# First-layer weights of two experts loaded as column halves over two depth blocks, the rest asked for behind two gathers

## The chip, the cores and the metric

The kernel runs on one core of one Trainium2 chip. The metric is the device time of one execution in microseconds, given as the median of several runs. Engines are PE (TensorE, matrix products), DVE (VectorE), ACT (ScalarE), POOL (GpSimd) and SP (SyncE, which only issues transfers here); transfers go through DMA queues.

## The reference

The kernel computes block-causal attention and feeds its result to a mixture of experts with fixed capacity:

```python
# attention: 8 batches, 8 heads, 576 positions of 64, blocks of 64
scores = scale * np.matmul(q, k.transpose(0, 1, 3, 2))
scores = np.where(block_i >= block_j, scores, -1000000000.0)
attn = softmax(scores)                      # exp(s - max) / (sum + 1e-9)
x = np.matmul(attn, v)                      # as x: 4608 tokens x 512
# mixture of experts: N=4608 tokens, D=512, E=8 experts, F=1024, cap=576
logits = x @ w_gate
for idx in np.argsort(-logits.flatten()):   # best (token, expert) pairs first
    tok, e = idx // E, idx % E
    if assigned[tok] < 0 and counts[e] < cap:
        assigned[tok] = e; counts[e] += 1
for e in range(E):
    h = np.maximum(x[assigned == e] @ w1[e], 0.0)
    out[assigned == e] = h @ w2[e]
```

`w1` is 8 x 512 x 1024 and `w2` 8 x 1024 x 512, in float32.

## The kernel before

The first 340 us are attention; its end writes x to DRAM as pairs of float16 values (a high and a low part), 1024 values a token, and leaves the gate's logits in SBUF. The rest is the mixture of experts, taken expert by expert (`k` = 0 to 7, in an order found while it runs).

For each expert but the last, `route` (L710) finds the logit that the 576th token has, by a search of 14 steps. A step is a loop over three engines: DVE makes three candidates (`cd`, L769) and counts with two of them (`jk`, L777), ACT counts with the third (`ja`, L750), a small matmul adds the counts over the partitions (`tot`, L791), and DVE turns them into the next step (`sg`, L794). Before the search PE transposes the logits (`rt`, L741) and ACT copies them to `m_PB` (L745). After it, `po` and `pe` (L852 and L908) and the DVE work between them (L870, L897, L899, L900) turn the chosen tokens into a list of indices `ix`, and a new expert's route may begin.

`gather` (L972) has POOL fetch the 576 rows of x in five indirect transfers `xg` (L980). For experts 0 and 1 `flip` has PE transpose each of them (`xt`, L990), and ACT and DVE copy the result to `X` (L994, L995); later experts use transposing transfers of SP (L1005).

`weights` (L927) fetches an expert's weights on SP's queue as eight pieces `raw` of 128 x 1024 float32, 512 KB each (L966), into six buffers. A piece of w1 (n = 0 to 3) is one block of 128 depths by all 1024 columns; a piece of w2 (n = 4 to 7) two blocks by 512 columns. `conv` splits each into two float16 parts, high and low. For w1 of experts 0 and 1 the high part is one instruction of ACT (L938) and the low part one of DVE (L940); for everything else ACT scales and rounds (L945, L949) and POOL subtracts (L951).

`ffn` (L1008) multiplies. For each group f of 128 columns of w1 and each of four depth blocks d it runs three matmuls `h` (L1030: high by high, high by low, low by high), for expert 0 first for 128 tokens, then for 448, for the others for 256 and 320. ACT takes the result out as `HH` (L1016) and DVE its low part as `HL` (L1018). Then `y` (L1055, L1059) multiplies with w2 for five groups of tokens; `yo` is scaled out and scattered to the output by POOL (L1046). Eight matmuls `warm` (L924) fill the wait for the first gather.

All engines' orders are fixed when the program is built. Each helper is a generator that yields the engine, a cost in ns and the events it needs; a list scheduler `Sched` picks the next by these, and the instructions are written out in that order. So an engine runs its list in sequence and waits in place. `sc.set` and `sc.soft` give the time of an event as the scheduler believes it; `hold` (L886) keeps `po` and `pe` of the last expert back by a fixed time in that schedule. The two lines that say what a set of h matmuls of expert 0 waits for, and what the first piece of w2 of expert 0 does, are

```python
yield T,3*(w/2.4+3),...,('wc',k,d) if k==0 else None      # L1026: depth block d converted
yield G,60,('gi',0); ... nc.gpsimd.memset(raw[:,0:1],0.0)  # L960-962
```

The memset of one column makes that piece's transfer wait for POOL, which runs it behind the fifth gather; SP's queue is in order, so the pieces after it wait too.

## Time and profile before

| | us |
|---|---|
| median of 3 runs | 804.21 |
| the runs | 802.95, 804.21, 807.38 |
| profiled execution, its own time | 801.86 |
| span of the profiled execution | 800.1 |
| PE busy | 717.8 (90%) |
| DVE busy | 585.0 (73%) |
| ACT busy | 545.1 (68%) |
| POOL busy | 467.0 (58%) |

Busy time of an engine is the sum over its instructions; what an engine lacks to the span is idle time, in front of some instruction, and the profile names what released it. The granted clock of PE is given in parts of its full 2.4 GHz. A transfer's time runs from its issue on a queue to its landing. Times below are from the start of the span.

### The profile page before, as it was taken

To read this page: it belongs to the slowest core of one execution; us is meant where nothing else is said; L and a number is where in the kernel's file an instruction comes from. 1 tells how busy PE (TensorE), PEld (TensorE's weight loads), DVE (VectorE), ACT (ScalarE), POOL (GpSimd) and SP (SyncE) were. 2 spreads that over 40 slices of the span, in tenths; PEclk is the share of its full clock that TensorE was granted. 3 is DMA by queue.
4 is the path that set the end of the run, shared out by engine and by line. 5 is a ranking of instruction groups with operands and counts; after the bars stand their busy time and mean duration, and the time that the engine had idled before them with its cause. 6 is when DMAs were issued, how large, how long until landed. Compare 5 with 4: busy or idle time off the path is not lost.

```text
span 800.1 us, 19136 instructions
## 1 busy us (share of the span) xinstructions
PE 717.8 (90%) x6539; PEld 479.6 (60%) x6539; DVE 585.0 (73%) x2395; ACT 545.1 (68%) x1476; POOL 467.0 (58%) x509
## 2 busy tenths in 40 slices
PE   5889998899999999913898999999999999999995
PEld 3666676677767767601644755747557475574752
DVE  6899798988889799488787977969777683730210
ACT  5789888888988888533745859496775947392210
POOL 5788888897889876212324337475471926873001
PEclk9899999999999999955899999999999999999998
DMA  9879999999999991324408049291845819861001
GB/s 203 157 145 179 213 203 209 164 176 204 230 164 222 188 198 35 99 80 133 138 14 294 25 139 231 74 295 42 254 129 184 179 49 273 270 162 40 20 15 45
DMA packets 244305, 121.51 MB, mean 152 GB/s; under 512 B 200816, under 2 KB 227312, under 8 KB 244208
## 3 DMA queue, kind: packets, MB, share of 16 engines
q1 hardware_dynamic: 238320, 101.42, 56.1%
q0 software_dynamic: 5888, 18.88, 7.4%
q8 instruction: 51, 0.84, 0.4%
q14 instruction: 46, 0.38, 0.2%
HBM read 71.32 MB, written 18.87 MB: 113 GB/s over the span
## 4 chain that ended last, share of the span: by engine, by line
PE 58%; DVE 19%; DMA 8%; ACT 8%; issue 3%; POOL 3%; SPq 1%; POOLq 0%; DVEq 0%; ACTq 0%
PE h L1030 23%; PE y L1055 16%; PE psb L463 5%; DVE m L405 5%; PE psb L380 4%; DMA kT<-k 4%; PE psb L498 4%; ACT P L416 4%; DVE kS L350 2%; POOL P L438 2%; PE y L1059 2%; DMA xg<-x,ix 2%; ACT PT L444 2%; DVE jk L776 1%; DMA raw<-in_moe_w_dram 1%
## 5 line engine op out<-in xcount | busy, mean ns | idle before, releaser
L438 POOL TENSOR_TENSOR P<-P,m 128x320 f32<-128x320 f32 (+8 forms) x285 | 209.3, 769 | 48.2 <-DVE m L430 28.4
L1030 PE MATMUL h<-X,W 128*128 128x320 f16 (+3 forms) x1536 | 195.1, 287 | 0.0
L1030 PEld LDWEIGHTS <-W 128*128 128x128 f16 x1536 | 142.2, 98 | 42.7 <-issue 3.1
L416 ACT ACTIVATE P<-psb,m 128x576 f32<-128x576 f32 (+8 forms) x288 | 149.2, 542 | 25.8 <-DVE m L409 19.7
L1055 PE MATMUL y<-W,HH 128*128 128x512 f16 x512 | 152.2, 379 | 0.0
L951 POOL TENSOR_TENSOR W<-raw,W 128x1024 f16<-128x1024 f32 x56 | 118.4, 2136 | 40.6 <-ACT W L949 38.3
L405 DVE TENSOR_REDUCE m<-psb 128x1 f32<-128x576 f32 (+8 forms) x288 | 125.0, 481 | 12.4 <-PE psb L380 11.9
L463 PE MATMUL psb<-mident,P 128*128 128x128 f32 x800 | 106.0, 281 | 10.9 <-POOL P L438 3.6
L1046 POOL DMA_INDIRECT out_dram<-yo,ix x40 | 39.4, 986 | 113.1 <-ACT yo L1038 79.2
L380 PEld LDWEIGHTS <-qT 128*64 128x64 f16 x1408 | 78.1, 112 | 42.8 <-issue 27.8
L380 PE MATMUL psb<-kT,qT 128*64 128x288 f16 (+8 forms) x704 | 91.7, 286 | 10.2 <-ACT P L416 9.7
L463 PEld LDWEIGHTS psb<-mident,P 128*128 128x128 f32 x800 | 87.3, 142 | 22.5 <-POOL P L438 6.4
L498 PE MATMUL psb<-PT,V 128*64 128x448 f32 (+5 forms) x776 | 97.2, 388 | 2.4 <-DVE PT L446 1.9
L980 POOL DMA_INDIRECT xg<-x,ix x40 | 41.6, 1040 | 95.8 <-DVE ix L918 37.7
L1055 PE MATMUL y<-W,HL 128*128 128x512 f16 x256 | 97.0, 379 | 0.0
L1016 ACT ACTIVATE HH<-h 128x320 f16<-128x320 f32 (+3 forms) x128 | 52.1, 410 | 63.9 <-PE h L1030 59.5
L444 ACT ACTIVATE PT<-psb 128x512 f32<-128x512 f32 (+1 forms) x165 | 82.4, 592 | 5.8 <-PE psb L463 5.6
L380 PE MATMUL psb<-kS,qT 128*64 128x288 f16 (+8 forms) x704 | 84.4, 284 | 1.6 <-DVE kS L350 1.5
L1018 DVE SCALAR_TENSOR_TENSOR HL<-h,HH 128x320 f16<-128x320 f32 (+3 forms) x128 | 56.9, 452 | 38.5 <-ACT HH L1016 38.2
L1055 PEld LDWEIGHTS <-HH 128*128 128x128 f16 x512 | 46.9, 98 | 52.6 <-issue 2.0
L945 ACT ACTIVATE raw<-raw 128x512 f32<-128x512 f32 x112 | 67.4, 626 | 6.6 <-DMA raw<-in_moe_w_dram 6.5
L498 PEld LDWEIGHTS psb<-PT,V 128*64 128x64 f32 x776 | 49.5, 137 | 33.5 <-issue 24.3
(204 smaller groups left out, 1074.9 us busy)
## 6 DMA issues: line engine op xcount, KB each, us to landing
raw<-in_moe_w_dram SPq DMA_DIRECT2D x64, 512.0 KB, 5.5
x<-XR SPq DMA_DIRECT2D x8, 1152.0 KB, 5.7
kn<-in_k_dram SPq DMA_DIRECT2D x15, 576.0 KB, 5.1
qn<-in_q_dram SPq DMA_DIRECT2D x15, 576.0 KB, 7.1
V<-in_v_dram SPq DMA_DIRECT2D x64, 128.0 KB, 4.4
V<-in_v_dram SPq DMA_DIRECT2D x16, 64.0 KB, 3.9
xg<-x,ix POOLq DMA_INDIRECT x40, 4.3
out_dram<-yo,ix POOLq DMA_INDIRECT x40, 2.8
```

Of the source, the lines that this page charges most:

```text
L380: nc.tensor.matmul(out if len(K1.shape) == 2 else out.rearrange("p (r j) -> p r j", r=2), lhsT=A[:, h, 64 * i:64 * i + 64], rhs=K1, start= ...
L405: nc.vector.tensor_reduce(m[:, 0, c:c + 1], ps[:, o:o + 64 * (i + 1)] if g else s.part(ps, g, i, o), axis=AX.X if g else AX.XY, op=OP.max)
L416: nc.scalar.activation(out, in_, AF.Exp, bias=m[:, 1, c:c + 1], scale=s.ESC, accum_out=m[:, 2, c:c + 1])
L438: nc.gpsimd.tensor_tensor(sl, sl, m[:, 3, c:c + 1].to_broadcast([P, w]), op=OP.mult)
L444: s.nc.scalar.activation(out, in_, AF.Copy)
L463: nc.tensor.transpose(ps[:, a], s.Pb[n % s.NP][:, s.OFF[i] + 128 * j:s.OFF[i] + 128 * j + P], s.ident)
L498: nc.tensor.matmul(ps[64 * h:64 * h + 64, 64 * (i0 - b0):64 * (b1 - b0)], lhsT=vn[:, j, 2 * (n % 2) + h, :], rhs=pt[:, s.PTI[(j, i0)]:s.PT ...
L945: nc.scalar.activation(raw[:,x],raw[:,x],AF.Copy,scale=s.WS)
L951: nc.gpsimd.tensor_tensor(lw,raw,hi,op=OP.subtract)
L1018: nc.vector.scalar_tensor_tensor(HL[:,f,ts],ps,0.0,HH[:,f,ts],op0=OP.max,op1=OP.subtract)
L1030: nc.tensor.matmul(ps,lhsT=W[:,a,d,f*P:f*P+P],rhs=X[:,4*(d//2)+d%2+l,ts],start=(d==0 and n==0),stop=(d==3 and n==2))
L1055: if m<4: nc.tensor.matmul(ps,lhsT=Z[:,f,m*P:m*P+P],rhs=Y[:,a,f],start=(f==n==0),stop=(f==7 and n==2))
```

## The change

For experts 0 and 1 a piece of w1 is no longer one depth block by 1024 columns but two depth blocks by 512 columns, as w2's are: pieces 0 and 1 together are columns 0 to 511 over all four depth blocks (f = 0 to 3), pieces 2 and 3 columns 512 to 1023 (f = 4 to 7). An h matmul waits for the piece that holds its depth blocks and columns. Piece 2 of both experts gets a memset on POOL, as piece 4 of expert 0 had, that waits for the new event `g1`, set when the second gather is issued. Pieces 6 and 7 of expert 2 wait for the end of that expert's transposes in the schedule. The scheduler is told 4600 ns instead of 1100 for how long a gather of expert 1 takes, and `hold` of the last expert goes from 8000 to 10000. The bytes moved, the matmuls and the conversions are the same.

```diff
@@ -885,7 +885,7 @@
         yield from s.invert(k,L16,h2)
     def hold(s,k):
 
-        s.sc.ev['hold',k]=s.sc.now+(8000 if k==s.E-1 else 0)
+        s.sc.ev['hold',k]=s.sc.now+(10000 if k==s.E-1 else 0)
     def invert(s,k,L16,h2):
         nc=s.nc; rp=s.rp; C=s.C; V=nc.vector; sc=s.sc
         yield D,440
@@ -936,38 +936,46 @@
             if k<2 and n<4:
                 yield A,947,('wl',k,n)
                 nc.scalar.activation(hi,raw,AF.Copy,scale=s.WS)
-                yield D,1135,('ix',k),('xm',0,0) if k==0 and n in s.XC else None
+                yield D,1135,('ix',k)
                 nc.vector.scalar_tensor_tensor(lw,raw,s.WS,hi,op0=OP.mult,op1=OP.subtract)
             else:
                 for h in range(2):
-                    x=slice(512*h,512*h+512)
                     yield A,520,('wl',k,n)
-                    nc.scalar.activation(raw[:,x],raw[:,x],AF.Copy,scale=s.WS)
+                    nc.scalar.activation(raw[:,h],raw[:,h],AF.Copy,scale=s.WS)
                 for h in range(2):
-                    x=slice(512*h,512*h+512)
                     yield A,520
-                    nc.scalar.activation(hi[:,x],raw[:,x],AF.Copy)
+                    nc.scalar.activation(hi[:,h],raw[:,h],AF.Copy)
                 yield G,2079
                 nc.gpsimd.tensor_tensor(lw,raw,hi,op=OP.subtract)
             sc.set(ev)
-        for dst,src,nd,wd in ((W,s.w1,4,1024),(Y,s.w2,8,512)):
-            g=1024//wd
-            for d in range(0,nd,g):
-                if n>=6: yield S,25,'hw',('wc',k,n-6)
-                elif k>0: yield S,25,'hw',('wc',k-1,n+2),('fl',1) if k==1 and n>=4 else None
-                elif n==4:
-
-                    yield G,60,('gi',0)
-                    raw=wp.tile([P,1024],F32,tag="raw",name=f"raw{k}_{wd}_{d}",bufs=6)
-                    nc.gpsimd.memset(raw[:,0:1],0.0)
-                    yield S,25,'hw'
-                else: yield S,25,'hw'
-                if k or n!=4: raw=wp.tile([P,1024],F32,tag="raw",name=f"raw{k}_{wd}_{d}",bufs=6)
-                nc.sync.dma_start(out=raw.rearrange("p (g f) -> p g f",g=g),in_=src[bass.ds(e,1),d*P:(d+g)*P,:].rearrange("o (g p) f -> p (o g) f",p=P))
-                hi=dst[:,0,d:d+g].rearrange("p g f -> p (g f)"); lw=dst[:,1,d:d+g].rearrange("p g f -> p (g f)")
-                sc.dma(1456,('wl',k,n))
-                sc.add(conv(n,raw,hi,lw,('wc',k,n)),2,sc.now)
-                n+=1
+        two=lambda t: t.rearrange("p (g f) -> p g f",g=2)
+        for n in range(8):
+            if n<4 and k<2:
+
+                d,c=2*(n%2),slice(512*(n//2),512*(n//2)+512)
+                src=s.w1[bass.ds(e,1),d*P:(d+2)*P,c]
+                hi,lw=[W[:,i,d:d+2,c] for i in range(2)]
+            elif n<4:
+                src=s.w1[bass.ds(e,1),n*P:(n+1)*P,:]
+                hi,lw=[two(W[:,i,n]) for i in range(2)]
+            else:
+                d=2*n-8
+                src=s.w2[bass.ds(e,1),d*P:(d+2)*P,:]
+                hi,lw=[Y[:,i,d:d+2] for i in range(2)]
+            tile=lambda: wp.tile([P,1024],F32,tag="raw",name=f"raw{k}_{n}",bufs=6)
+            behind={(0,2):('g1',0),(0,4):('gi',0),(1,2):('g1',1)}.get((k,n))
+            if behind:
+
+                yield G,60,behind,('wc',k-1,n+2) if k else None
+                raw=tile()
+                nc.gpsimd.memset(raw[:,0:1],0.0)
+            if n>=6: yield S,25,'hw',('wc',k,n-6),('fl',2) if k==2 else None
+            elif k>0: yield S,25,'hw',('wc',k-1,n+2),('fl',1) if k==1 and n>=4 else None
+            else: yield S,25,'hw'
+            if not behind: raw=tile()
+            nc.sync.dma_start(out=raw.rearrange("p (g f) -> p g f",g=2) if n>3 or k<2 else raw.rearrange("p (g f) -> p g f",g=1),in_=src.rearrange("o (g p) f -> p (o g) f",p=P))
+            sc.dma(1456,('wl',k,n))
+            sc.add(conv(n,two(raw),hi,lw,('wc',k,n)),2,sc.now)
     WS=32.0; XS=64.0; NWU=8; NWM=0; GW=1; GS=2; XC=()
     def gather(s,k,ix):
         nc=s.nc; fp=s.fp; sc=s.sc
@@ -978,9 +986,11 @@
             if m==0: X=s.X[k]=fp.tile([P,8,576],F16,tag="X",name=f"X{k}")
             xg=fp.tile([P,1024],F16,tag="xg",name=f"xg{k}_{m}",bufs=5)
             nc.gpsimd.indirect_dma_start(out=xg[:n],out_offset=None,in_=s.xd,in_offset=bass.IndirectOffsetOnAxis(ap=ix[:n,m:m+1],axis=0))
-            sc.soft(728,('xg',k,m))
+
+            sc.soft(728,('xg',k,m),4600 if k==1 else 1100)
             sc.nolat()
             if m==4: sc.set(('gi',k))
+            if m==1: sc.set(('g1',k))
             sc.add(s.flip(k,m,n,xg,X),1,sc.now)
     def flip(s,k,m,n,xg,X):
         nc=s.nc; sc=s.sc
@@ -1007,7 +1017,7 @@
         if m==4: sc.set(('fl',k))
     def ffn(s,k):
         nc=s.nc; fp=s.fp; sc=s.sc
-        yield S,0,('xm',k,0),('xm',k,1 if k else 0),*[('wc',k,n) for n in range(4) if k or n==0]
+        yield S,0,('xm',k,0),('xm',k,1 if k else 0),*[('wc',k,n) for n in range(4) if k>1 or n<=k]
         (W,Y),X=s.W[k],s.X[k]
         HH=fp.tile([P,8,576],F16,tag="HH",name=f"HH{k}",bufs=1); HL=fp.tile([P,8,576],F16,tag="HL",name=f"HL{k}",bufs=1)
         def hev(f,h,ps,gk,ts):
@@ -1023,7 +1033,7 @@
                 pg={}
                 nf=4 if k==0 and h==0 and f0==0 else 1
                 for f,d in [(f,d) for a in range(f0,f0+4,nf) for d in range(4) for f in range(a,a+nf)]:
-                    yield T,3*(w/2.4+3),'g' if d==0 else None,('g2',k-1),*[('xm',k,m) for m in range(1,5) if h],('wc',k,d) if k==0 else None
+                    yield T,3*(w/2.4+3),'g' if d==0 else None,('g2',k-1),*[('xm',k,m) for m in range(1,5) if h],('wc',k,2*(f//4)+d//2) if k<2 else None
                     if d==0: gk=sc.gtake(); pg[f]=s.ps.tile([P,512],F32,tag="g",name=f"h{k}_{f}_{h}",bufs=4)[:,:w],gk
                     ps,gk=pg[f]
                     for n,(a,l) in enumerate(((0,0),(0,2),(1,0))):
```

The scheduler turns this into other orders. `raw_n` is the buffer of piece n, `sg_t`, `cd_t`, `jk_t` and `tot_t` belong to step t of the search, `h_f` to column group f, `xt_m` and `xg_m` to gather m. Three places, all at the start of expert 0 beside the search of expert 1:

DVE before, from the first low part of w1 (L940) to the second of the copies of X:

```order
L940 SCALAR_TENSOR_TENSOR W_0_5523<-raw_1024_0_5536,W_0_5523 128x1024
L940 SCALAR_TENSOR_TENSOR W_0_5523<-raw_1024_1_5541,W_0_5523 128x1024
L719 TENSOR_REDUCE m_vm<-m_Lm 128x36
L723 MEMSET SC_5635 128x2
L735 TENSOR_TENSOR m_nP<-m_Lm,m_vm 128x288
L940 SCALAR_TENSOR_TENSOR W_0_5523<-raw_1024_2_5545,W_0_5523 128x1024
L737 SCALAR_TENSOR_TENSOR PV_5638<-m_nP,m_Lm 128x288
L995 COPY X_5622<-xt_0_5644 128x4x128
L940 SCALAR_TENSOR_TENSOR W_0_5523<-raw_1024_3_5551,W_0_5523 128x1024
L995 COPY X_5622<-xt_1_5657 128x4x128
```

DVE after, first from the first count of the search on, then around `sg_2`:

```order
L777 TENSOR_SCALAR jk_0_0_5741,cn_0_5739<-m_PB,bs_5720 128x288
L777 TENSOR_SCALAR jk_0_1_5747,cn_0_5739<-m_PB,bs_5720 128x288
L1005 COPY X_5618<-xt_3_5729 128x4x128
L794 SCALAR_TENSOR_TENSOR sg_0_5776<-tot_0_5763,m_wk 128x3
L940 SCALAR_TENSOR_TENSOR W_0_5523<-raw_2_5634,W_0_5523 128x2x512
L769 TENSOR_SCALAR cd_1_5779<-CB_5719,sg_0_5776 128x1 x3
L777 TENSOR_SCALAR jk_1_0_5796,cn_1_5778<-m_PB,cd_1_5779 128x288
L777 TENSOR_SCALAR jk_1_1_5800,cn_1_5778<-m_PB,cd_1_5779 128x288
L779 TENSOR_SCALAR CB_5719<-CB_5719,sg_0_5776 128x1
```

```order
L1028 SCALAR_TENSOR_TENSOR HL_5666<-h_2_0_5695,HH_5665 128x128
L1028 SCALAR_TENSOR_TENSOR HL_5666<-h_3_0_5701,HH_5665 128x128
L794 SCALAR_TENSOR_TENSOR sg_2_5839<-tot_2_5835,m_wk 128x3
L940 SCALAR_TENSOR_TENSOR W_0_5523<-raw_3_5640,W_0_5523 128x2x512
L769 TENSOR_SCALAR cd_3_5842<-CB_5719,sg_2_5839 128x1 x3
L777 TENSOR_SCALAR jk_3_0_5854,cn_3_5841<-m_PB,cd_3_5842 128x288
```

The low parts of pieces 2 and 3, which stood ahead of the search, now stand behind `sg_0` and behind `sg_2`.

POOL after, from the first gather of expert 0 (before, the five gathers and one memset stood in a row):

```order
L988 DMA xg_0_5619<-x,ix_5607 128x1024
L988 DMA xg_1_5623<-x,ix_5607 128x1024
L988 DMA xg_2_5626<-x,ix_5607 128x1024
L971 MEMSET raw_2_5634 128x1
L988 DMA xg_3_5638<-x,ix_5607 128x1024
L988 DMA xg_4_5652<-x,ix_5607 64x1024
L971 MEMSET raw_4_5667 128x1
```

A memset for piece 2 came between the third and the fourth gather; expert 1's gathers now have the same memset in the same place.

PE after, around the count `tot_2` of that search, with what an instruction waits for (`DVE_49` is DVE's semaphore):

```order
L791 LDWEIGHTS m_bo [waits DVE_49]
L791 MATMUL tot_2_5835<-cn_2_5811,m_bo 128x3 [waits Activation_49]
L1040 LDWEIGHTS W_0_5523
L1040 MATMUL h_4_0_5816<-X_5618,W_0_5523 128x128
L1040 LDWEIGHTS W_0_5523
L1040 MATMUL h_4_0_5816<-X_5618,W_0_5523 128x128
L1040 LDWEIGHTS W_0_5523 [waits DVE_49]
L1040 MATMUL h_4_0_5816<-X_5618,W_0_5523 128x128
```

The weights that wait are those of the low part of piece 3. Ahead of them PE has the 48 h matmuls of f = 0 to 3 and eight of `h_4`; before, 39 matmuls of `h_4` to `h_7` stood between `tot_1` and `tot_2`, with no such wait. In the next stage, PE's transposes of expert 1's gathers stand behind 30 `y` matmuls from the `rt` of expert 2 on, where there were 18, and from `po` to `pe` of the last expert there are 42 `y` matmuls of full width, 24 of `y_4` and 12 of h instead of 51 `y`.

## Rows read from the trace of the kernel before

**Rows 1.** The page: busy time, share of the span, instructions.

```profile
PE   717.8 (90%) x6539; PEld 479.6 (60%) x6539; DVE 585.0 (73%) x2395; ACT 545.1 (68%) x1476; POOL 467.0 (58%) x509
```

**Rows 2.** PE's waits, us in total, times, longest: 366 to 446, then 446 to 800.

```profile
PE xt L990 <- DMA xg<-x,ix: 7.4, 6, 2.3
...
PE tot L791 <- ACT ja L750: 1.1, 1, 1.1
...
PE pe L908 <- DVE RH L900: 1.3, 1, 1.3
PE tot L791 <- ACT ja L750: 1.3, 2, 0.7
```

**Rows 3.** Timeline of PE, 378 to 392: start, us, what, idle before.

```profile
379.84 1.04 PE L990 MATMUL xt<-m_idh,xg 128*128 128x128 f16 x8 [0.49 <-DMA xg<-x,ix]
...
382.74 1.81 PE L1030 MATMUL h<-X,W 128*128 128x128 f16 x15
...
385.19 0.63 PE L741 MATMUL rt<-mident,PV 128*128 128x128 f32 x2
...
387.51 0.17 PE L791 MATMUL tot<-cn,m_bo 128*128 128x3 f16 x1
...
389.65 2.34 PE L1030 MATMUL h<-X,W 128*128 128x128 f16 x39
```

**Rows 4.** PE in windows of 1 us: busy, granted clock, DMA share, GB/s.

```profile
380.00:381.00 1.00, 0.87 (x8) 0.50 0.72 164
...
386.00:387.00 1.00, 1.00 (x19) 0.80 1.05 408
```

**Rows 5.** Groups by form, 372 to 450: busy us, mean ns, idle before.

```profile
L940 DVE SCALAR_TENSOR_TENSOR W<-raw,W 128x1024 f16<-128x1024 f32 x8 | 9.7, 1222 | 1.0 <-ACT W L938 1.0
...
L995 DVE COPY X<-xt 128x512 f16<-128x512 f16 x8 | 3.4, 422 | 6.4 <-ACT X L994 6.4
```

**Rows 6.** Timeline of DVE, a step of the search.

```profile
387.74 0.16 DVE L794 SCALAR_TENSOR_TENSOR sg<-tot,m_wk 128x3 f32<-128x3 f32 x1 [0.16 <-PE tot L791]
...
389.32 0.48 DVE L1018 SCALAR_TENSOR_TENSOR HL<-h,HH 128x128 f16<-128x128 f32 x2
389.71 0.15 DVE L794 SCALAR_TENSOR_TENSOR sg<-tot,m_wk 128x3 f32<-128x3 f32 x1
```

**Rows 7.** Timeline of POOL, third and fourth gather of expert 0.

```profile
377.59 1.92 POOL L980 DMA_INDIRECT xg<-x,ix  x1 [0.30 <-issue]
379.82 0.95 POOL L980 DMA_INDIRECT xg<-x,ix  x1 [0.30 <-issue]
```

**Rows 8.** DMA issues at 369.2, 424.5 and 430.7: KB, us to landing.

```profile
raw<-in_moe_w_dram SPq DMA_DIRECT2D x1, 512.0 KB, 3.6
...
raw<-in_moe_w_dram SPq DMA_DIRECT2D x1, 512.0 KB, 8.9
...
xg<-x,ix POOLq DMA_INDIRECT x1, 7.8
```

**Rows 9.** Timeline of PE, 434 to 440.

```profile
434.86 0.62 PE L990 MATMUL xt<-m_idh,xg 128*128 128x128 f16 x8 [1.75 <-DMA xg<-x,ix]
...
436.29 0.62 PE L990 MATMUL xt<-m_idh,xg 128*128 128x128 f16 x8 [0.81 <-DMA xg<-x,ix]
...
438.53 0.62 PE L990 MATMUL xt<-m_idh,xg 128*128 128x128 f16 x8 [0.97 <-DMA xg<-x,ix]
439.08 0.62 PE L1059 MATMUL y<-W,HH 128*64 128x512 f16 x4
```

**Rows 10.** Chain that ended last, 678 to 694, then the timeline of POOL.

```profile
677.80 2.37 PE y L1055 x11
...
680.55 5.26 DVE h L870
...
686.48 5.31 DVE OL L897
...
679.46 6.30 POOL L951 TENSOR_TENSOR W<-raw,W 128x1024 f16<-128x1024 f32 x3
```

## Prediction, made before the changed kernel was run

> **What bounds the kernel now.** I read the page first: PE is busy for 90% of the span [rows 1], so a change that adds no PE work can only win or lose waits and clock. PE's waits come next, cut at 446 us, because the moved instructions end there. In 366 to 446 us PE waits 7.4 us for gathered rows of x, in six places, and 1.1 us for a count of the search; in all the rest of the MoE part it waits 1.3 us for RH and 1.3 us for counts [rows 2]. So there are three places to price. Stage A (376 to 394 us) is where expert 0's gathers, its first matmuls and the start of expert 1's search meet. Stage B (428 to 444 us) is the same meeting for experts 1 and 2. The third is `pe` of the last expert. Everywhere else PE works back to back, and there the same matmuls cost the same.
>
> In stage A the reader should see PE's timeline [rows 3]: transposes `xt` with waits between them, the first `h` matmuls at 382.74, `rt` at 385.19, the first count `tot` at 387.51, and from 389.65 on an unbroken run. The clock goes with that: 1.2 GHz (granted 0.50) in 380 to 381 us, after a stretch in which PE had only scattered transposes, and 0.80 as the mean of 386 to 387, which puts the return to 2.4 GHz at about 386.4 [rows 4].
>
> **Stage A, the start.** The change puts `h_0`, `h_1` ahead of the transposes of the third gather. The second transposes start at 379.84 and take 1.04 at the low clock [rows 3]; their gather is late because POOL wrote its descriptors beside a DVE subtraction, and the two subtractions that overlap it stay where they are. So the first h matmul moves from 382.74 to about 380.9: 1.9 us earlier. `rt` now stands behind eight more transposes (1.04) and 21 h matmuls; 15 of these took 1.81 us in the row [rows 3], so 21 take 2.3 at this clock, and `rt` starts at 384.2, a microsecond earlier. Its copy and the ACT count follow, and `tot_0` comes at about 386.1 instead of 387.51. None of this is a gain yet, since PE order is fixed and the next thing in it decides.
>
> **Stage A, the new wait.** Before, all four low parts of w1 (DVE, 1.22 us each [rows 5]) are done before the search starts. After, piece 2's stands behind `sg_0` and piece 3's behind `sg_2`, both on the loop DVE to PE to DVE that the search is; and PE's order has only 8 matmuls of `h_4` that can run before piece 3's low part, of 48 for f 4 to 7. So PE stands until DVE gets there. A search step, from one `sg` to the next, takes 1.97 us, with two HL evictions (0.48) in it [rows 6]. From `tot_0` at 386.1: `sg_0` 0.16, piece 2's low part 1.22, the rest of a step 1.81, a step with two more HL 2.45, `sg_2` 0.16, piece 3's low part 1.22: 7.0 us, so PE goes on at 393.1. In the trace of before PE reached that matmul, the ninth of a run of 39 in 2.34 us from 389.65 [rows 3], at 390.1. That is **+3.0 us**. Everything behind it is PE work to the next stage.
>
> Its bounds hang on when piece 2 lands, which ACT converts ahead of the copy of `rt`. It is asked for behind the third gather. That gather began at 377.59 and took 1.92 beside a DVE subtraction that is now gone; alone such an instruction takes 0.95 [rows 7], so it ends at 378.5, and with the memset behind it SP asks at about 378.8 (my estimate). A piece took 3.6 us with nothing else on its way and 8.9 at worst [rows 8]. I take 4, nearest to the first row because only two gathers run beside it. It must have landed by about 383.8 for its ACT half (a microsecond, by DVE's 1.22 [rows 5]) to be done as `rt` is, so up to 5.0 us cost nothing; at 8.9 the loss is 3.9 us more. Below, the term goes to +2.0 if one HL pair and an `sg` overlap.
>
> **Stage A, the clock.** Between 386.1 and 393.1 PE has 17 h matmuls, a set of transposes and three counts, some 2 us of work in 7. In the stretch before 380 it was about as sparse and the clock fell. I expect 0.50 again. Before, PE worked without a gap at that level from 382.74 to 386.4 [rows 3, 4], and half of these 3.7 us was lost; I take the same once more: **+1.8 us**. Bounds 0 (it holds) and +3.6 (it falls twice).
>
> **Stage B.** Here PE waits for gathers three times, 1.75, 0.81 and 0.97 us, 3.5 in all [rows 9]; in this stage a gather took 7.8 us to land [rows 8], with six pieces of expert 1's weights asked for just ahead. After, only two are. The gathers then need about 3.6, the row of a transfer with little beside it [rows 8], and are there before PE comes: PE's order has 30 more y matmuls after `rt` before the first transposes where there were 18, and three of them take 0.65 us. New waits for the search come in exchange. From `tot_2` to `tot_3`, and from `tot_3` to `tot_4`, PE has two sets of transposes (0.62 each [rows 9]) and three y: 1.9 us. DVE needs a step without HL, 1.97 - 0.48 = 1.5 [rows 6], and two copies of X, 0.42 each [rows 5]: 2.3. I make that 0.4 a time, 0.8 in all, and the 3.5 us become 0.8: **-2.7 us**. Bounds: 0, if the gathers meet pieces 2 to 7, asked for in one go behind the third gather, and -3.5, if the counts hide.
>
> **The last expert.** `hold` moves `pe` back. Between `po` and `pe` stood 51 y matmuls; eleven take 2.37 [rows 10], so 11.0 us, and PE waited 1.3. Now 42 such, 24 `y_4` and 12 narrow h stand there: 9.0 us, 3.1 us (four `y_4` take 0.62 [rows 9], with overlap about half a full y each) and 1.4 us (as in [rows 3], at twice the columns and the clock), 13.5 in all. The chain beside it is 11.0 + 1.3 = 12.3 us, of which two DVE instructions take 5.26 and 5.31, beside POOL subtractions back to back [rows 10]. So the wait goes: **-1.3 us**. One more such stretched instruction makes the chain 17.6 and the wait 4.1, the upper bound +2.8. Row and skill differ here. The row shows a small DVE instruction held for 5.26 us beside three POOL subtractions of 2.1 each. The Trainium skill (SBUF — State Buffer, "SBUF: two separate sides") says that the shared port pair is an exclusive lock which whoever starts first keeps for the whole instruction; by that DVE would wait for one subtraction at most, the chain would be some 6 us shorter, and this wait of 1.3 would not have been there to remove; the sum would be +2.1. I go by the row.
>
> **At no cost.** The memset between the third and fourth gather delays the fourth by less than one gather's 0.95 [rows 7]; `xt_3` stands behind 18 h matmuls. Expert 1's pieces 4 to 7 land up to 8 us later; y of expert 1 comes some 29 us after its first h. The wait of pieces 6 and 7 of expert 2 for the transposes is covered by that expert's whole h. If one of these covers fails, POOL's low part (2.1 each) is what y waits for. The 1.3 us of waits for counts later [rows 2] may fall or double; I take 0.
>
> **Sum.** +3.0 + 1.8 - 2.7 - 1.3 = +0.8. The profiled execution took 801.86, so 802.7; the median of the runs shown is 804.21, 2.35 above it, so **805.0**. Half a per cent is 4.0 us, about what a measurement of this kernel tells from no change: faster means under 800.2, slower over 808.2.
>
> **Rivals.** *The head start is kept.* If PE does not stop at `h_4` and the clock never falls, stage A gives -1.9 and -1.8, and with -2.7 and -1.3 the time is 796.5. For it speaks that the gathers have the queues nearly to themselves; against it, that DVE's fixed order puts the low part behind two search steps. Between the two (+3.0 stays, clock holds) lies 803.2. *Piece 2 lands late, slower.* At 8.9 us [rows 8] it lands at 387.7, holds ACT's copy of `rt` and so the whole search, and the sum is +4.7: 808.9. It decides from 5.0 us after the request and passes 808.2 at 8.2. For it speaks that two gathers and piece 3 are beside it and that such times stand in the trace; against it, that nearly all of them belong to six pieces at once. *It does not do what it says.* The held pieces only collide with the gathers behind them: stage B gives 0 and the time is 807.7. For it speaks the 7.8 us gather; against it, that three of the five are out before the memset.
>
> **How the numbers follow.** My forecast 0.50; the head start kept 0.18; late piece 0.15; no relief in stage B 0.13; the rest 0.04. The last-but-one is mostly within 4 us, and the forecast's own bounds (clock 0 to 3.6, piece 3.6 to 8.9) spill a little on both sides: faster 0.20, same 0.57, slower 0.23. For the range I cut a tenth at either side: 798.5, between the kept head start and 803.2, and 809.5, just over the late piece.
>
> **What would show it.** Right: the first h matmul near 381; PE's waits with a new line h or its weight load behind DVE's low part, about 1.5 us long, and two or three for counts, in 386 to 394; a granted clock of 0.5 somewhere in 388 to 397; the waits of `xt` for DMA after 420 gone, small waits of `tot` for DVE in their place; no wait of the last `pe`. Wrong: PE unbroken from 381 on, or `tot_0` later than 388, or xt waits over 1 us in stage B.

## The result and the profile after

The changed kernel takes 808.48 us as the median of 20 runs (802.82 to 811.83); the kernel before, run beside it, takes 804.35 (800.41 to 807.89). The ratio is 1.0048, with a 95% interval of 1.0030 to 1.0066. That is 3.9 us slower, from 2.4 to 5.3 (the medians themselves differ by 4.1): inside the range of the forecast, within its half per cent, and 3.5 us above the time it gave. The profiled execution took 809.18 us with a span of 807.4, so the two profiled spans differ by 7.3 us, more than the medians do. Where these 7.3 us went is shown first, and then which part of them stays when more executions are looked at.

PE's waits after, 366 to 446 us and then to the end, answer to [rows 2]; us in total, times, longest:

```profile
PE xt L1000 <- DMA xg<-x,ix: 4.9, 4, 1.9
PE tot L791 <- DVE jk L777: 3.0, 3, 1.9
...
PE h L1040 <- DVE W L940: 1.3, 1, 1.3
...
PE h L1040 <- DVE HL L1028: 0.5, 1, 0.5
...
PE tot L791 <- ACT ja L750: 3.8, 3, 3.1
```

The gathers cost less, the search and the weights more, and the last `pe` (1.3 in [rows 2]) has gone. The new line h behind `W` L940 is the one that the prediction named. PE's timeline after, 379 to 400, answers to [rows 3]:

```profile
379.98 0.85 PE L1040 MATMUL h<-X,W 128*128 128x128 f16 x6
...
385.71 0.62 PE L1000 MATMUL xt<-m_idh,xg 128*128 128x128 f16 x8 [1.41 <-DMA xg<-x,ix]
...
387.01 0.17 PE L791 MATMUL tot<-cn,m_bo 128*128 128x3 f16 x1
...
389.93 0.18 PE L791 MATMUL tot<-cn,m_bo 128*128 128x3 f16 x1 [1.89 <-DVE jk L777]
...
392.00 0.19 PE L791 MATMUL tot<-cn,m_bo 128*128 128x3 f16 x1 [0.94 <-DVE jk L777]
...
393.74 2.85 PE L1040 MATMUL h<-X,W 128*128 128x128 f16 x25 [1.31 <-DVE W L940]
```

The first h comes at 379.98 (before 382.74), but `tot_0` at 387.01 is only 0.5 us earlier, because the fourth gather's transposes at 385.71 are late. The matmul that stood at 390.1 before stands at 393.74. DVE's timeline after, around `sg_0` and `sg_2`:

```profile
387.34 0.15 DVE L794 SCALAR_TENSOR_TENSOR sg<-tot,m_wk 128x3 f32<-128x3 f32 x1
...
387.42 1.22 DVE L940 SCALAR_TENSOR_TENSOR W<-raw,W 128x1024 f16<-128x1024 f32 x1
...
392.38 0.15 DVE L794 SCALAR_TENSOR_TENSOR sg<-tot,m_wk 128x3 f32<-128x3 f32 x1
...
392.46 1.22 DVE L940 SCALAR_TENSOR_TENSOR W<-raw,W 128x1024 f16<-128x1024 f32 x1
```

The two low parts stand in the search, and the second ends as h goes on. The clock, in PE's windows of 1 us (busy, granted clock, DMA share, GB/s):

```profile
383.00:384.00 1.00, 1.00 (x11) 0.50 0.99 383
384.00:385.00 1.00, 0.30 (x3) 0.57 1.04 244
...
391.00:392.00 1.00, 0.06 (x2) 0.84 0.00 0
392.00:393.00 1.00, 0.42 (x3) 0.50 0.00 0
...
397.00:398.00 1.00, 1.00 (x12) 0.50 0.00 0
398.00:399.00 1.00, 1.00 (x7) 0.75 0.00 0
```

It returned to 2.4 GHz in the slice at 384 (before at 386.4), fell again in that at 391, behind a stretch with long waits, and was back in that at 398. From 393.74 to about 398.5 PE worked without a gap at half speed: 2.4 us lost. The 3.6 us by which that matmul is late and these 2.4 make 6.0, about what stage A lost (5.8 in the table below).

DMA issues after, in 378.1 to 378.3 us (POOL's fourth gather, and piece 2 asked for 0.16 us ahead of it), and in 435.7 to 435.8, the same in stage B; us to landing at the end:

```profile
raw<-in_moe_w_dram SPq DMA_DIRECT2D x1, 512.0 KB, 4.9
xg<-x,ix POOLq DMA_INDIRECT x1, 7.5
...
raw<-in_moe_w_dram SPq DMA_DIRECT2D x1, 512.0 KB, 4.1
xg<-x,ix POOLq DMA_INDIRECT x1, 8.1
```

The held pieces land soon; the gathers beside them do not. In stage A the second and third gather, issued ahead of the held piece, took 3.4 and 3.9, and the fourth of the kernel before, at 379.8, took 3.5:

```profile
xg<-x,ix POOLq DMA_INDIRECT x1, 3.4
...
xg<-x,ix POOLq DMA_INDIRECT x1, 3.9
...
xg<-x,ix POOLq DMA_INDIRECT x1, 3.5
```

What is asked for behind piece 2 is slow too: the fifth gather took 6.6 us, and pieces 3 to 6 took 6.7 to 8.2.

In PE's timeline of stage B (answering to [rows 9]) the first three sets of transposes no longer wait for a transfer, and the fourth waits longer than any did before:

```profile
438.42 1.05 PE L1000 MATMUL xt<-m_idh,xg 128*128 128x128 f16 x16
...
443.94 0.62 PE L1000 MATMUL xt<-m_idh,xg 128*128 128x128 f16 x8 [1.94 <-DMA xg<-x,ix]
```

And at 637.57 there is a wait that nobody expected. ACT's row, then two of PE:

```profile
635.82 0.63 ACT L944 ACTIVATE raw<-raw 128x512 f32<-128x512 f32 x1 [3.79 <-DMA raw<-in_moe_w_dram]
...
637.57 0.16 PE L791 MATMUL tot<-cn,m_bo 128*128 128x3 f16 x1 [3.07 <-ACT ja L750]
...
638.83 1.06 PE L1065 MATMUL y<-W,HH 128*128 128x512 f16 x2
```

A piece of a later expert lands late, ACT stands at its conversion, the search's count stands behind that in ACT's fixed order, and PE behind the count. Behind the stall two y matmuls take 1.06 us instead of 0.59: the lower clock again (granted 0.50 from 638 to 640).

To compare executions I cut each profiled span at four points of PE's work, which hold the same 1536 h matmuls in every kernel: the first `warm`, the end of expert 0's last h (192nd), of expert 1's 96th (288th) and of expert 5's last (1152nd). Each figure is a difference of two such times in the trace:

```
us                     warm      A: to     B: to     middle: to  end     span
                       starts    h 192     h 288     h 1152
before                 372.91    38.09     43.49     215.98      129.60  800.1
changed                373.02    43.90     42.73     219.49      128.28  807.4
difference             +0.11     +5.81     -0.76     +3.51       -1.32   +7.3
before, again          375.24    38.61     43.31     219.33      133.08  809.6
changed, again         373.06    46.84     42.67     224.60      129.59  816.8
```

### The profile page after: what moved, and what is told of

The parts are those of the page before. It is cut to its first block, busy times and chain, and to the rows that moved or that the text cites. A ratio compares the mean times of both kernels' runs of the same rounds, so it can differ in the third digit from the quotient of the medians.

```text
span 807.4 us, 19137 instructions
## 1 busy us (share of the span) xinstructions
PE 720.6 (89%) x6539; PEld 480.9 (60%) x6539; DVE 584.4 (72%) x2395; ACT 547.3 (68%) x1476; POOL 465.3 (58%) x511
## 4 chain that ended last, share of the span: by engine, by line
PE 52%; DVE 20%; DMA 10%; ACT 7%; issue 5%; POOL 4%; SPq 0%; POOLq 0%; DVEq 0%; ACTq 0%
PE y L1065 18%; PE h L1040 17%; PE psb L463 5%; DVE m L405 5%; DMA kT<-k 4%; PE psb L498 4%; PE psb L380 4%; ACT P L416 3%; PE y L1069 2%; POOL P L438 2%; DMA xg<-x,ix 2%; DVE kS L350 2%; DMA raw<-in_moe_w_dram 2%; ACT PT L444 1%; DVE jk L776 1%
## 5 line engine op out<-in xcount | busy, mean ns | idle before, releaser
L1040 PE MATMUL h<-X,W 128*128 128x320 f16 (+3 forms) x1536 | 198.9, 290 | 1.8 <-DVE W L940 1.3
L1040 PEld LDWEIGHTS <-W 128*128 128x128 f16 x1536 | 145.1, 100 | 44.7 <-issue 3.6
L380 PE MATMUL psb<-kT,qT 128*64 128x288 f16 (+8 forms) x704 | 89.8, 282 | 11.2 <-ACT P L416 10.5
L988 POOL DMA_INDIRECT xg<-x,ix x40 | 39.6, 990 | 89.0 <-DVE ix L918 78.0
L380 PE MATMUL psb<-kS,qT 128*64 128x288 f16 (+8 forms) x704 | 82.1, 278 | 0.6 <-DVE kS L350 0.5
```

Of the source, the lines that this page charges most:

```text
L380: nc.tensor.matmul(out if len(K1.shape) == 2 else out.rearrange("p (r j) -> p r j", r=2), lhsT=A[:, h, 64 * i:64 * i + 64], rhs=K1, start= ...
L1040: nc.tensor.matmul(ps,lhsT=W[:,a,d,f*P:f*P+P],rhs=X[:,4*(d//2)+d%2+l,ts],start=(d==0 and n==0),stop=(d==3 and n==2))
```

## The experiments

All figures with an interval are ratios to runs of the kernel before on the same chip, in twelve or fewer runs each; on those chips it took 809.5 to 809.9 us. They are not quotients of two medians, which can differ by 0.002 (before_hold 0.9959, after_again 1.0056). The stretches are those of the table. (Where an expectation gives bounds for a stretch, they came from a rougher count, which for A reads some 0.5 us lower than the table.)

My theory: stage A loses by the search that has the low parts in it, and by the clock; stage B gains little because the fourth gather meets the held pieces; hold gives what it should. The rivals are the shape of the pieces, and the wait at 637 us.

**no_hold_e0.** One entry of `behind` is left out, so expert 0's pieces are asked for at once:

```diff
-            behind={(0,2):('g1',0),(0,4):('gi',0),(1,2):('g1',1)}.get((k,n))
+            behind={(0,4):('gi',0),(1,2):('g1',1)}.get((k,n))
```

> The change without the hold of expert 0's piece 2 (its four pieces of w1 are asked for at once, still as column halves; expert 1's stay held). PE and DVE then run the start of expert 0 in the order of the kernel before, the four low parts ahead of the search. Theory (the 5.6 us that stage A lost are the low parts of pieces 2 and 3 standing in the search, and the clock that falls in the wait): no wait of h for W in stage A, tot_0 near 387.5, the first 448-column matmul within 1 us of before; what is left is stage B (-0.7) and the last expert (-1.3), so some 802 us, ratio to before 0.995 to 1.000. Rival 1 (the pieces by columns or the gathers cost it, not the order): stage A stays 3 us or more late, ratio 1.003 to 1.007. Rival 2 (the loss is the wait for a count at 637 us, behind a late piece of a later expert): that wait of about 3 us stays in the trace and the ratio stays over 1.002.

Ratio 1.0034 (1.0014 to 1.0055). Stage A is as before, 38.16 us: the first rival's part about the shape is out, and the loss there comes from the hold of expert 0 and what follows from it. The ratio missed, because stage B took 48.64. PE's timeline there:

```profile
450.05 0.17 PE L791 MATMUL tot<-cn,m_bo 128*128 128x3 f16 x1
452.59 0.18 PE L791 MATMUL tot<-cn,m_bo 128*128 128x3 f16 x1 [2.37 <-DVE jk L777]
...
453.85 2.83 PE L1040 MATMUL h<-X,W 128*128 128x256 f16 x13 [0.84 <-DVE W L940]
```

With expert 0 moved, the scheduler laid stage B out anew and put two counts with nothing between them, ahead of the low part of expert 1's piece 3: in this run the pattern that stage A has in the changed kernel is in stage B. An earlier count there waits 2.65 us for DVE (438.95). Of the second rival's wait at 637 us 0.9 is left, at 639.6.

**no_hold_e1.** The other entry is left out:

```diff
+            behind={(0,2):('g1',0),(0,4):('gi',0)}.get((k,n))
```

> The change without the hold of expert 1's piece 2 (expert 0's stays). Stage A is in the order of the changed kernel. Theory: stage A is 5.6 us late as there, with a wait of h for W of about 1.3 us and the clock at 0.5 around 392 to 398; in stage B the gathers wait beside six pieces again, 3 to 4 us in all as before, or are hidden behind a moved order; last expert -1.3. Sum +4 to +5 us, ratio 1.004 to 1.007. Rival (stage B is what made the change slower): ratio 1.000 or below.

Ratio 1.0071 (1.0046 to 1.0097), as expected. A 43.95 with the wait for `W` at 1.3 again, B 43.06. Expert 0's hold alone carries the loss of stage A, and in stage B expert 1's hold is worth no more than some tenths of a microsecond.

**low_first.** The low parts of expert 0's pieces 2 and 3 get the highest rank, so DVE makes them ahead of `sg_0`:

```diff
-            sc.add(conv(n,two(raw),hi,lw,('wc',k,n)),2,sc.now)
+            sc.add(conv(n,two(raw),hi,lw,('wc',k,n)),-1 if k==0 and 2<=n<4 else 2,sc.now)
```

> The change, with the low parts of expert 0's pieces 2 and 3 given the highest rank in the schedule, so that DVE makes both ahead of the first sg and not behind sg_0 and sg_2; the holds stay. Theory: no wait of h for W is left; the search starts when piece 3 has landed and been converted, so tot_0 comes at about 388 and tot_1 at about 390 with PE waiting some 2 us there, and 48 h matmuls follow without a gap. Stage A is then 1 to 2.5 us late instead of 5.6, and the time falls by 3 to 4.5 us from the change's, to 803 to 806 us, ratio 0.999 to 1.002. Rival 1 (arrival of the pieces, not DVE's order): stage A stays about 5 us late, ratio 1.004 or more.

Ratio 0.9991 (0.9968 to 1.0015), as expected, but not by the expected way. The wait of h for `W` is gone, yet stage A is still 42.55, 4.5 us late where 1 to 2.5 was expected, only 1.4 less than in the changed kernel; where the rest of the gain came from is not shown. PE's timeline of this run:

```profile
388.00 1.03 PE L1000 MATMUL xt<-m_idh,xg 128*128 128x128 f16 x8 [1.92 <-DMA xg<-x,ix]
...
394.35 0.17 PE L791 MATMUL tot<-cn,m_bo 128*128 128x3 f16 x1 [2.10 <-ACT ja L750]
```

The fourth gather holds PE here too, and the search starts later for it (`tot_0` at 392.07, where 388 was expected). So there is a second cause in stage A, the collision that I had looked for in stage B alone.

**before_hold.** The kernel before with one number changed:

```diff
-        s.sc.ev['hold',k]=s.sc.now+(8000 if k==s.E-1 else 0)
+        s.sc.ev['hold',k]=s.sc.now+(10000 if k==s.E-1 else 0)
```

> The kernel before with hold of the last expert at 10000 and nothing else. Theory: the wait of the last pe for RH (1.3 us) is gone, everything ahead of it as before; -1.3 us, ratio 0.997 to 1.000. Rival (the order that this moves makes another wait): a new wait of PE after 690 us and a ratio of 1.000 or more.

Ratio 0.9944 (0.9923 to 0.9964): 4.5 us faster (2.9 to 6.2; by the medians 3.3), where 1.3 was expected. The wait is gone and the end takes 128.57 us. No kernel of the study has a lower ratio, though the intervals of two others overlap with its own.

**before_again.** The kernel before, for a second profile.

> The kernel before, unchanged, for a second profile of it. Every theory: ratio 1.000 within its interval. What is read from it is the last pe's wait for RH (1.3 us in the first profile; if hold alone is worth 4.5 us, it should be 3 to 5 us here) and the waits for counts between 480 and 650 us (1.3 us in the first profile; 4 to 6 us if the difference between the runs comes from there).

Ratio 0.9990 (0.9974 to 1.0007). It accounts for the 4.5: its end takes 133.08 us, 4.5 more than that of before_hold, and the wait of the last `pe` is twice that of the first profile. PE's row, and the window of 700 to 705:

```profile
700.02 0.92 PE L908 MATMUL pe<-RH,OL 128*32 128x40 f16 x36 [2.73 <-DVE RH L900]
...
700.00:705.00 5.00, 4.98 (x68) 0.66 0.73 229
```

Behind the wait the granted clock is 0.66 on average over 5 us, some 1.7 us of lost work. Wait and clock together are 4.4. The middle, too, took 3.4 us more than in the first profile, with waits for counts of 1.2, 1.7 and 0.8 us in it, 3.8 in all, a little under the 4 to 6 that the expectation set.

**after_again.** The changed kernel, for a second profile.

> The changed kernel, unchanged, for a second profile of it. Theory (the loss of stage A is set by the order, the wait of 3.1 us at 637 us is not): stage A the same within 0.5 us (tot_0 near 387, h waits for W 1.3 us, the clock at 0.5 around 392 to 398), the fourth gather of expert 1 waits about 2 us again, and the counts between 480 and 650 wait in other places and by other amounts. Ratio 1.003 to 1.007. Rival (the wait at 637 us is part of the change): it stands there again with about 3 us.

Ratio 1.0038 (1.0016 to 1.0060), as expected. But stage A was 2.9 us longer still, so the theory's half microsecond failed: the fourth gather made PE wait 3.44 us and `tot_0` came at 390.48.

```profile
388.06 1.04 PE L1000 MATMUL xt<-m_idh,xg 128*128 128x128 f16 x8 [3.44 <-DMA xg<-x,ix]
...
390.48 0.21 PE L791 MATMUL tot<-cn,m_bo 128*128 128x3 f16 x1
...
445.07 0.17 PE L791 MATMUL tot<-cn,m_bo 128*128 128x3 f16 x1 [1.41 <-ACT ja L750]
...
446.87 0.62 PE L1000 MATMUL xt<-m_idh,xg 128*128 128x128 f16 x8 [0.52 <-DMA xg<-x,ix]
```

In stage B (the last two rows) the fourth gather cost 0.52 us and not the 2 that were expected; a count waited 1.41 instead, and the stretch took 42.67, the same as in the first profile.

At 638 us the wait was 1.2 instead of 3.1, so the 3.1 is not set by the order, with others of 2.1, 1.9 and 2.2 at 494, 588 and 645.

**hold_8000.** The changed kernel with hold back at 8000.

> The changed kernel with hold of the last expert back at 8000. Theory: the wait of the last pe for RH comes back, 1.3 us as in the first profile of the kernel before or up to the 4.5 us that hold alone gave there; the rest as in the changed kernel; ratio to the kernel before 1.006 to 1.012. Rival (hold is worth nothing, the gain of that run was its middle experts): ratio as the changed kernel, 1.003 to 1.006, and no wait of pe over 0.5 us.

Ratio 1.0099 (1.0082 to 1.0116), in six runs. The last `pe` waits 2.62 us again and the end takes 133.72. PE's row:

```profile
704.87 0.92 PE L908 MATMUL pe<-RH,OL 128*32 128x40 f16 x36 [2.62 <-DVE RH L900]
```

From both sides, hold was worth 4.5 to 4.9 us by the ratios and 3.3 to 3.7 by the medians, and it hid as much of the loss of stage A.

**e1_behind_all.** Expert 1's piece 2 behind all five gathers:

```diff
+            behind={(0,2):('g1',0),(0,4):('gi',0),(1,2):('gi',1)}.get((k,n))
```

> The changed kernel with expert 1's piece 2 behind all five of its gathers, not behind three. Theory (the 2 us that are left of the waits in stage B are the collision of the fourth gather with pieces 2 to 7): no wait of xt for a gather over 0.5 us after 430, expert 1's first h 1.5 to 2.5 us earlier than in the changed kernel measured from its rt, ratio lower than the changed kernel's by 0.002 to 0.003, if the later pieces do not make a new wait of h for W. Rival (the fourth gather is late for itself): its wait stays near 2 us.

Ratio 1.0036 (1.0015 to 1.0057). No transposes of stage B wait for a gather any more; stage B falls to 42.01, only 0.7 us under the changed kernel's, since a count waits 1.4 us in its place. ACT's rows, then PE's:

```profile
442.12 0.60 ACT L1004 ACTIVATE X<-xt 128x512 f16<-128x512 f16 x1 [2.47 <-PE y L1065]
442.61 0.56 ACT L750 ACTIVATE ja<-m_PB,cd 128x324 f16<-128x324 f32 x1
...
443.31 0.16 PE L791 MATMUL tot<-cn,m_bo 128*128 128x3 f16 x1 [1.38 <-ACT ja L750]
```

In ACT's order a copy of X stands ahead of the count and waits for PE. The ratio does not move. How much of the fourth gather's wait the collision makes is less sure here than in stage A: with expert 1's piece behind three gathers, as in the changed kernel, it was 1.9, 0.5 and 0.6 us (hold_8000) and nothing in low_first, whose stage B took 42.03.

**both_all.** Piece 2 of both experts behind all five gathers:

```diff
+            behind={(0,2):('gi',0),(1,2):('gi',1)}.get((k,n))
```

> The changed kernel with piece 2 of both experts behind all five gathers. Theory (part of what stage A lost is the fourth gather of expert 0, which lands 7.5 to 8.7 us after its issue because the held pieces are asked for right beside it): no wait of xt for the fourth gather over 0.5 us in stage A, all five gathers landed by 384; piece 2 and 3 land some 2 us later than in the changed kernel, and the low part of piece 3, now ahead of sg_2, still stops h. From the first warm matmul to the last h of expert 0 40 to 41.5 us, against 42.6 to 46.2 in the profiles with the change's order and 37.5 to 38.0 before; ratio 1.000 to 1.003. Rival (the fourth gather is late for itself, or DVE's order is all): this stretch stays at 42.5 us or more.

Ratio 1.0025 (1.0000 to 1.0050). The fourth gather's transposes stand in stage A at 381.88 without a wait, and `tot_0` at 385.05, two microseconds ahead of the changed kernel:

```profile
381.88 1.03 PE L1000 MATMUL xt<-m_idh,xg 128*128 128x128 f16 x8
...
385.05 0.17 PE L791 MATMUL tot<-cn,m_bo 128*128 128x3 f16 x1
...
392.06 3.17 PE L1040 MATMUL h<-X,W 128*128 128x128 f16 x28 [0.49 <-DVE W L940]
```

A is 42.20, between what theory and rival gave, against 43.0 to 46.8 in the five profiles with the change's order. In all six profiles in which expert 0's piece 2 stands behind three gathers, PE waits for the fourth, 0.9 to 3.4 us; here and in both_all_low, with the piece behind all five, it does not. The head start goes into two counts that wait 2.5 and 1.9 us for ACT. Piece 2, asked for later, lands later, and ACT converts it and piece 3 ahead of the first of them:

```profile
385.79 1.06 ACT L938 ACTIVATE W<-raw 128x1024 f16<-128x1024 f32 x1 [1.02 <-DMA raw<-in_moe_w_dram]
```

So the longer hold has a price of its own.

**both_all_low.** The edits of both_all and low_first together.

> As the run above, with the low parts of expert 0's pieces 2 and 3 also given the highest rank (DVE makes both right behind sg_0). Theory (gather and DVE's order are the two halves of the loss): no wait of h for W over 0.5 us, no wait of xt over 0.5 us; what stays is the search held up once by some 2.4 us of low parts and the wait for the pieces; 39 to 40.5 us for the stretch, ratio 0.997 to 1.001. Rival (the clock at its lower level in this stretch is the loss, whatever waits go): 42 us or more.

A is 40.57, as expected: 38.1 before, 43.9 in the changed kernel, 42.20 with the gathers freed, 40.57 with the low parts out of the way as well. Wait of h for `W` in stage A: none. The ratio missed, 1.0060 (1.0039 to 1.0082) in six runs: stage B, laid out anew, lost more than A gained (44.14, with a wait of 1.25 for `W` of expert 1), though not enough for the whole of the miss. The 2.5 us that stage A still lacks are not taken apart by a run of their own; in this trace `tot_1` waits 2.60 us while DVE makes both low parts.

**e0_free_e1_all.** Expert 0 without hold, expert 1 behind all gathers, and another guess for the scheduler:

```diff
+            behind={(0,4):('gi',0),(1,2):('gi',1)}.get((k,n))
...
-            sc.soft(728,('xg',k,m),4600 if k==1 else 1100)
+            sc.soft(728,('xg',k,m),2800 if k==1 else 1100)
```

> A version meant to beat both: expert 0's pieces of w1 asked for at once (no hold), expert 1's behind all five gathers, the scheduler told 2800 ns for a gather of expert 1 instead of 4600, hold 10000. Theory: the stretch to the last h of expert 0 as before (37.5 to 38.0 us); from there to the last of the first 96 h of expert 1 42 to 42.5 us against 43.5 before; the last pe without a wait. Ratio 0.990 to 0.995. Rival (what was measured of hold alone, 0.994, is all there is to be had): 0.994 to 0.997, and stage B no shorter than 43 us.

Ratio 0.9961 (0.9941 to 0.9980). It beats both kernels, but by no more than hold alone, and so the rival is right: A 37.80, end 128.52, but B 43.79, no better than before. No transposes there wait for a transfer; one set waits 1.34 us for a copy of X, and h 0.89 us for `W` of the held pieces.

**layout_only.** No new hold, and the gather time back, so that PE and DVE are in the order of the kernel before, with the pieces as column halves:

```diff
+            behind={(0,4):('gi',0)}.get((k,n))
...
+            sc.soft(728,('xg',k,m),1100)
```

> The pieces of experts 0 and 1 as column halves, none of the new holds, the scheduler's gather time back at 1100, hold 10000: PE's and DVE's orders in both stages are those of the kernel before. Theory (the shape of the pieces costs and gives nothing, only what is held and what order follows does): both stretches as before within 0.5 us (37.5 to 38.0 and 43.5), ratio as hold alone, 0.993 to 0.997. Rival (pieces of 2 KB rows land later than those of 4 KB): stage A or B longer by over 1 us and the ratio 0.998 or more.

Ratio 0.9953 (0.9927 to 0.9979), the same as hold alone within the intervals. A 37.37, B 43.76: the shape of the pieces costs nothing and gives nothing that can be measured.

## Why the prediction was right where it was, and where it failed

*The new wait in stage A (+3.0)* was right in mechanism and in size: h goes on at 393.74 where 393.1 was forecast, 3.6 us late. It came about by another path, though. The start was earlier than forecast (379.98, not 380.9), since the second gather's instruction was no longer stretched (0.98 us, not 1.73), which the forecast had not reckoned with and which the second profile does not repeat (1.99, first h at 380.61); piece 2 was asked for at 378.03 and took 4.9 us, inside the 5.0 that cost nothing. What ate the lead was the fourth gather, 1.41 us of PE's time, of which the prediction said that it was covered by 18 h matmuls ("at no cost", at most 0.95 late). That is the step that failed in stage A: I priced POOL's instruction behind the memset, and not the transfer that the memset lets loose beside it. both_all shows it: without the collision, no wait there.

*The clock (+1.8)* was right: 2.4 GHz was lost between 391 and 398.5, which cost 2.4 us. Together A was to lose 4.8 and lost 5.8, in a second profile 8.2.

*Stage B (-2.7)* was wrong: -0.8, -0.6 in the second profile. Its upper bound was the rival "it does not do what it says", and that is what happened, in the first profile for the reason given there: pieces 2 to 7, asked for in one go, meet the fourth gather, which takes 8.1 us. That is one half of the failure. The other is the 0.4 us that I had set for a count. In the second profile the gather cost 0.5 and a count 1.4, and freed from the collision (e1_behind_all) stage B gives 1.3 and not 2.7, with a count that waits 1.4. I had reckoned with DVE's step and its copies of X alone; ACT's count, behind its own copy of X, came later than that.

*The last expert (-1.3)* was right in sign, exact in the first pair of profiles and far too small later: hold alone gave 4.5. The term was mis-sized in two ways. The wait in the one profile that I had was a small one (1.3; 2.6 and 2.7 elsewhere), and I counted only the wait, though in stage A I had counted the clock behind one: 2.7 of wait and 1.7 of clock in before_again. In the first profile the granted clock stayed at 1.00 behind the wait, so the exact hit was that profile's luck. Whether chip or execution decides between the two is not shown. (In the same sum 24 `y_4` at half a full y each are 2.6 us and not 3.1; the cover of 13.0 still exceeds 12.3.) Of the Trainium skill's rule on the shared port (SBUF — State Buffer, "SBUF: two separate sides"), by which that wait should hardly exist, more below.

*The middle (0)* is open. In the first pair it took 3.5 us more. Four profiles with the order of the kernel before give 216.0 to 222.6 (mean 219.5), the ten others 219.5 to 225.2 (mean 222.8); the sets overlap, the waits stand at other places in each, and no run was made that changes the middle alone. PE's waits over 0.3 us there add up to 1.3 to 5.3 us in the four and 3.1 to 7.7 in the ten. It is not shown that the change makes it longer.

*Signs and rivals.* Of the signs of being right, the line h behind DVE's low part and the clock at 0.50 came, and the last `pe` no longer waits. One sign of being wrong came too, a wait of xt over 1 us in stage B (1.94), and in the second profile `tot_0` later than 388 (390.48). The bound for piece 2 was read too low: 8.9 was called the worst, but the trace of before has a piece that took 10.9, at 425.2. It did not matter, since piece 2 took 4.9.

The time came inside the range, with a stage A that was worse, a stage B that was hardly better, as in the rival "it does not do what it says" (807.7, with a chance of 0.13), and a last expert that on the later chips paid back more. By the ratio it is 3.9 us slower, where the sum said 0.8. In the profiled pair stage B alone missed by 1.9 us and stage A by 1.0, and the 3.5 of the middle were not in the sum at all; that the total came near it does not show that each term was right.

## What to carry to other kernels

A transfer that is held back so as not to disturb others has to stand behind the last of them, or the ones behind it pay: look at what a release lets loose, not at what its own instruction costs. Then it lands later itself, and what needs it pays (both_all). A conversion that left the head of a dependent loop went into the loop here, and there it cost PE its own length, and the clock behind the wait. And one profile shows one value of a wait: two edits in one change can hide each other, as 4.5 us from one number did here.

## What the runs showed of the hardware that was not expected

A small DVE instruction can be held for as long as several POOL instructions take. DVE and then POOL in before_again:

```profile
686.58 6.71 DVE L870 TENSOR_SCALAR h<-q 128x36 f16<-128x36 f32 x1
...
693.88 0.75 DVE L897 TENSOR_TENSOR OL<-m_iom,L 128x1152 f16<-128x1152 f16 x1
...
694.99 4.97 DVE L900 TENSOR_SCALAR RH<-OH,m_pc 128x720 f16<-128x720 f16 x1
...
685.90 1.01 POOL L1046 DMA_INDIRECT out_dram<-yo,ix  x1 [1.62 <-ACT yo L1038]
686.94 6.30 POOL L951 TENSOR_TENSOR W<-raw,W 128x1024 f16<-128x1024 f32 x3
...
694.04 1.47 POOL L1046 DMA_INDIRECT out_dram<-yo,ix  x1 [0.80 <-ACT W L949]
695.54 4.21 POOL L951 TENSOR_TENSOR W<-raw,W 128x1024 f16<-128x1024 f32 x2
```

`h` starts at 686.58, while POOL runs a scatter (685.90 to 686.91), and POOL's three subtractions follow the scatter without a gap; `h` ends at 693.29, when they have ended (693.24). `RH` starts at 694.99, in the next scatter (694.04 to 695.51), and ends at 699.96, with the two subtractions that run to 699.75. `OL`, which took 5.31 in the first profile [rows 10], starts between the two runs of POOL's and takes 0.75. So the instruction that is stretched is not always the same one, and it waits for a whole run of POOL's. The Trainium skill (SBUF — State Buffer, "SBUF: two separate sides") gives the pair of ports to whoever starts first, for the whole of that instruction. In both cases POOL was at work when DVE's instruction began, so who gives way does not speak against it; that DVE waited for three and four of POOL's instructions, and not for one, does.

A gather that was issued 0.16 us behind a 512 KB piece took 7.5 us to land in stage A, where gathers issued ahead of the piece took 3.4 and 3.9, and 8.1 in stage B, where they took 4.3. The piece itself took 4.9 and 4.1. The gather lost about what such a piece takes, but the pieces asked for behind it were on their way as well and were as slow; which of them it waited for is not shown.
